# Scores behind the w_in products: one engine order in the last two slots of a period

## The chip, the cores and the metric

The kernel runs on one core of a Trainium2 chip. The core has a matrix engine (TensorE, PE), a vector engine (VectorE, DVE), a scalar engine (ScalarE, ACT), GpSimd (POOL) and SyncE (SP), which issues transfers. Each engine works through its own instructions in the order in which the program gives them, and waits on semaphores where it needs another engine's result. The metric is the time of one execution in microseconds (us); of several executions the median is taken.

## The reference

The input is q, k and v of 8 batches, 8 heads, 576 tokens and 64 dimensions, and the weights w_in (512 x 2048) and w_out (2048 x 512). An approximate attention with 32 landmarks per head is followed by a layer with the activation SiLU:

```python
q_lm = q.reshape(B, H, m, S // m, D).mean(axis=3)      # m = 32 landmarks
k_lm = k.reshape(B, H, m, S // m, D).mean(axis=3)
A, Bm, C = sm(q, k_lm), sm(q_lm, k_lm), sm(q_lm, k)    # softmax of scaled scores
Z = Bm.T / (norm1(Bm) * norminf(Bm) + 1e-06)
for _ in range(6):
    Z = 2 * Z - Z @ Bm @ Z
x = (A @ Z @ C @ v)                                    # heads side by side: 4608 x 512
h = x @ w_in
out = (h / (1 + exp(-h))) @ w_out
```

## The kernel before

The kernel never forms x. For each batch it multiplies the small product Z C v (zwT, 64 x 32 per head) with w_in, which gives a matrix mb of 256 rows and 2048 columns, and then computes h as A times mb. A's softmax needs its scores, which are formed transposed: landmarks against tokens.

The work is cut into eight **periods**, one for each batch b, and each period into sixteen **slots** s. In a slot the kernel forms one sixteenth of h of batch b (`l1_mm`: four matmuls into a tile hps), applies SiLU to it on ScalarE (`l1_act`, line 807, into gT), and runs a few matmuls of the output product (`l2_mm`: ops, 16 matmuls for one block of 128 tokens, then a copy to ost on ScalarE and a transfer). How many ops matmuls a slot gets is written by hand in `CNT` and `REST`. Beside this, a period carries the attention of batch b + 1 (called `a`) through its steps, and prepares batch b + 2 (called `ready`). The schedule is manual: what the program writes first for an engine, that engine does first. The variable d is 2 and 3 in the first two periods and 0 from b = 2 on.

The steps that the change and the prediction touch, for b from 2 to 5:

- Slot 3: a one-word copy on GpSimd (`gate`, line 1139) holds GpSimd until the vector engine has written wsp. After it GpSimd sums landmarks of batch b + 2 (`landmarks_pool`, lines 229 to 237, in slots 4 and 8; the last result is lmn), between them it normalises A (`a_mul`, line 691) and issues the loads of v.
- Slots 7 to 12: four transposes of q and k of batch b + 2 on the vector engine (`transpose_qk`, line 203, into qkT).
- Slots 9 and 14: `a_back` (line 707) transposes the two halves of A of batch b + 1 on the vector engine; the second half is used from slot 8 of the next period.
- Slots 11 and 13: `m_pair` (line 757) forms two of the four column blocks of mb for batch b + 1. Each block is 8 matmuls on 64 x 32 tiles of TensorE. The first block (mp) lies in two banks of PSUM, row half 0 in pool psa and row half 1 in pool psn, and the vector engine casts it (line 773); the second (mpp) lies in a two-bank buffer of pool psh, and ScalarE casts it (line 774).
- Slot 13: `ready = Att(b + 2)` is made, and `lm_t` (line 271) transposes its landmarks lmn into lmc on the vector engine.
- Slot 15: three ops matmuls, then `ready.a_pair` (line 621): 32 score matmuls on 32 x 32 tiles into two psh buffers (sa), two transposes by the vector engine (line 626, into xs) and two reductions for the maxima (line 630, into nm). In slot 0 of the next period GpSimd subtracts them (`a_sub`), and in slot 2 ScalarE takes the exponential.

PSUM is shared out tightly: psh has two buffers of two banks, used in turn by hps, mpp, sa and the scores scp of slot 1; psa and psn have one bank each. psn holds the tile bb of the Newton steps from slot 1 to slot 10 and mp's row half 1 later. A buffer is written again only when its last reader is done.

Of the kernel before, what the change touches and what calls it, by code (L numbers as in the profile page):

```python
# [11 lines left out]
OP = mybir.AluOpType  # L12
AX = mybir.AxisListType
# [30 lines left out]
def kernel(  # L44
# [9 lines left out]
    nc = tc.nc  # L54
    B, H, S, Dh = q.shape
    L = 32
# [187 lines left out]
    class Att:  # L244
# [373 lines left out]
                   .to_broadcast((pr, 8 * n, L)), start=False, stop=True)  # L618


        def a_pair(self):
            self.a_first()
            for i in range(2):
                self.a_scores(i)
            for i in range(2):
                nc.vector.transpose(  # L626
                    out=self.xs[:, i],
                    in_=self.sa[i][:, :, 0:HF].rearrange("p r (t n) -> p r t n", n=L))
            for i in range(2):
                nc.vector.tensor_reduce(out=self.nm[:, i], in_=self.xs[:, i], op=OP.max,  # L630
                                        axis=AX.X, negate=True)
# [122 lines left out]

        def m_pair(self, f):
            self.m_done = f + 2
            if f == 0:
                mb_t[self.b] = attp.tile([128, 2, DFF], BF, tag="mb", name="mb")  # L760
            m = [psa1("mp"), psn1("mp")]
            m2 = ps2("mpp")
            for i in range(2):
                for j in range(4):
                    for r in range(2):
                        p = slice(64 * r, 64 * r + 64)
                        mm((m2[:, r, :] if i else m[r])[32 * j:32 * j + 32, :],
                           self.zwT[p, j, :],
                           w_in_sb[p, j, 512 * (f + i):512 * (f + i) + 512],
                           start=True, stop=True)  # L770
            o = mb_t[self.b][:, :, 512 * f:512 * f + 1024]
            for r in range(2):
                nc.vector.tensor_copy(out=o[:, r, 0:512], in_=m[r])  # L773
            nc.scalar.copy(out=o[:, :, 512:1024], in_=m2)  # L774

# [59 lines left out]
    def l2_add(b, *blocks):  # L837
        for i in blocks:
# [4 lines left out]

    CNT = {0: [0, 0, 0, 0, 4, 4, 2, 4, 4, 4, 2, 2, 2, 2, 1, 1],
           1: [2, 2, 2, 5, 2, 10, 9, 0] + [4] * 8,
           2: [8, 4, 12, 12, 3, 3, 2, 2, 3, 3, 3, 3, 3, 2, 2, 7]}
    REST = [3, 4, 12, 12, 3, 2, 2, 2, 4, 4, 4, 3, 3, 3, 3, 8]


    ORD = (1, 0, 3, 2)  # L850
# [86 lines left out]
    for b in range(B):  # L937
# [4 lines left out]
        a, ready = ready, None  # L942

        d = (2, 3)[b] if b < 2 else 0
        mp = (11, 13) if d == 0 else (14, 15)

        def l1(s):
            h[s] = l1_mm(b, s)
# [4 lines left out]
        for s in range(NDC):  # L953
# [63 lines left out]
            elif s == d + 2 and a.sub:  # L1017
                a.a_start()
                a.c_max(1)
                a.c_exp(0)  # L1020
                a.c_exp(1)
                a.a_exp_all()
                a.b_norm()
                l2_mm(cnt[s])
                table(AF.Silu)
                l1(s)
            elif s == d + 2:
                n = cnt[s]
                a.a_start()
                a.a_scores(0)  # L1030
                a.a_scores(1)
                a.c_max(1)
                a.a_max(0)
                a.a_max(1)
                a.c_exp(0)
                a.c_exp(1)
                a.a_scores(2)
                a.a_max(2)
                for i in range(2):
                    a.a_shift(i)  # L1040
                    a.a_exp(i)
                a.b_norm()
                a.a_shift(2)
                a.a_exp(2)
                table(AF.Silu)
                a0.m_unit(2, nc.vector.tensor_copy, nc.vector.tensor_copy, pair=True)
                a.c_transpose(0)
                a.c_out(0)
                load_v(2)
                a0.a_norm(1)  # L1050
                a0.a_norm(2)
                a.f_mm()
                a.b_scale()
                a.f_out()
                l2_mm(n)
                l1(s)
            elif b == 0:
                l1(s)
                r = s - d
                n = cnt[s]  # L1060
                if r == 3:
                    load_qk(3, (1,))
                    act(s - 1)
                    a0.m_unit(3, nc.scalar.copy, nc.scalar.copy, parts=2,
                              between=lambda: act(s))
                    nc.vector.tensor_tensor(out=parity, in0=mask[:, 0:2, 0],
                                            in1=mask[:, 2:4, 0], op=OP.add)
                elif r == 4:
                    a.ns_mm()
                    a.ns_step()  # L1070
                    act(s)
                    a0.a_transpose(1)
                    a0.a_out(nc.scalar.copy)
                    a.c_transpose(1)
                    a.c_out(1)
                    a.a_norm(0)
                    load_qk(3, (0,))
                elif r == 5:
                    act(s)
                    a.ns_mm()  # L1080
                    a.ns_step()
                    a.w_scale()
                    a.a_norm(1)
                elif r == 6:
                    a.ns_mm()
                    a.ns_step()
                    act(s)
                    l2_mm(2)
                    n -= 2
                    a.ns_mm()  # L1090
                    a.a_norm(2)
                    a.ns_step()
                    load_qk(3, (3,))
                elif r == 7:
                    a.ns_mm()
                    a.ns_step()
                    act(s)
                    l2_mm(2)
                    n -= 2
                    a.w_mm()  # L1100
                    a.w_out()
                    a.ns_mm(last=True)
                    a.x_out()
                    load_qk(3, (2,))
                    landmarks_pool(2, 0)
                elif r == 8:
                    a.z_mm()
                    a.z_out()
                    act(s)
                    l2_mm(n)  # L1110
                    n = 0
                    landmarks_pool(2, 2)
                    a.a_transpose(0)
                    a.a_out(nc.vector.tensor_copy)
                elif r == 10:
                    a.a_transpose(1)
                    a.a_out(nc.vector.tensor_copy)
                    transpose_qk(2, ORD[1])
                elif r > 11:
                    transpose_qk(2, ORD[r - 10])  # L1120
                if s in h:
                    act(s)
                if r in (9, 11):
                    a.m_pair(r - 9)
                if r == 9:
                    transpose_qk(2, ORD[0])
                l2_mm(n)
            elif s == d + 3:
                l1(s)
                act(s - 1)  # L1130
                act(s)
                l2_mm(2)
                a.f_mm()
                a.b_scale()
                a.f_out()
                a.w_scale()


                nc.gpsimd.tensor_copy(out=gate, in_=a.wsp[:, 0, :])  # L1139
                l2_mm(cnt[s] - 2)  # L1140
                a.ns_mm()
            elif s <= d + 8:
                l1(s)
                if s == d + 6:
                    a.w_mm()
                a.ns_step()
                act(s)
                if s == d + 4:
                    a.a_sum(0)
                elif s == d + 5:  # L1150
                    a.a_sum(1)
                elif s == d + 6:
                    a.w_out()
                    a.a_rec(0, 2)
                    a.a_mul(0)
                    a.a_mul(1)
                l2_mm(cnt[s])
                a.ns_mm(last=(s == d + 8))
            elif s == d + 9:
                l1(s)  # L1160
                a.x_out()
                act(s)
                l2_mm(cnt[s])
            elif s == d + 10:
                l1(s)
                a.z_mm()
                a.z_out()
                act(s)
                l2_mm(cnt[s])
            else:  # L1170
                l1(s)
                act(s)
                if nxt and s in mp:
                    a.m_pair(2 * mp.index(s))
                n = cnt[s]
                if s == 15 and ready and ready.early:
                    l2_mm(3)
                    n -= 3
                    ready.a_pair()
                l2_mm(n)  # L1180
            if b == 0:
                if s == 3:
# [1 line left out]
            elif b + 2 < B:  # L1184
# [16 lines left out]
                if s == 15 and b == 1:  # L1201
                    ready = Att(b + 2)
                    ready.lm_t(0, 2)
            back = (9, 14) if d == 0 else (12, 13)
            if nxt and b and s in back:
                a.a_back(back.index(s))
            if (b, s) == (0, 3):
# [34 lines left out]
```

## Time and profile before

| | |
|---|---|
| time, median of 3 executions | 260.57 us |
| lowest and highest | 260.43 and 260.59 us |
| the profiled execution, its own time | 260.7 us |
| its span, first to last instruction | 259.0 us |
| granted clock of TensorE | 1.00 over the whole span |
| mean time of one ops matmul in the records | 373 ns (they overlap; the work's pace is 216 ns) |
| one SiLU of a slot (line 807) | 652 ns |
| one cast of mp on the vector engine (line 773) | 684 ns |
| one cast of mpp on ScalarE (line 774) | 1012 ns |
| one transpose of a score half (line 626) | 762 ns |

The profile is of one execution. Busy time of TensorE counts matmuls that overlap, so it is not a measure of its peak; the pace of a group is read from the starts of its neighbours. In the timeline a line gives the start, the time from the first start to the last end, the engine, the line of the kernel, the tiles (written <- read), the shape, how many instructions are merged, and in brackets the idle time of the engine ahead of it with what ended it. All matmuls are recorded at one helper line, 80, so they are told apart by their tiles. A few per cent of the matmul records can be missing.

### The profile page before, as it was taken

The page shows a single profiled execution, that of the slowest core. Times are in us where ns is not written, and L with a number is a line of the kernel's source. Part 1 is how long each engine was busy: PE and PEld are TensorE (multiplying, and loading weights), DVE is VectorE, ACT ScalarE, POOL GpSimd, SP SyncE. Part 2 cuts the span into 40 slices and gives each one's busy share as a digit, 9 for nine tenths or more (in the row PEclk, how much of TensorE's full clock was granted, in tenths as well). Part 3 has the DMA queues.
Part 4 walks back from the last instruction along what each step waited for, and adds up shares of the span by engine and source line. Part 5 has one row for each costly group of instructions (what it writes and reads, how often), then busy time and mean ns, then how long its engine had stood idle before and what let it go on. Part 6 is the DMA issues. An engine that isn't in the chain of part 4 may idle for free.

```text
span 259.0 us, 6520 instructions
## 1 busy us (share of the span) xinstructions
PE 241.9 (93%) x2676; PEld 137.7 (53%) x2717; DVE 168.3 (65%) x396; ACT 169.9 (66%) x313; POOL 133.2 (51%) x161
## 2 busy tenths in 40 slices
PE   8879878999898999999999999999999999999994
PEld 2646544564554555556655564556545665556553
DVE  5878988769895969777885788776967645000000
ACT  2378964587846786779575957597668858445511
POOL 7707546983799469945993299319923030100000
PEclk9999999999999999999999999999999999999999
DMA  7999999970479982895289518134621500111122
GB/s 221 199 209 208 207 205 211 226 153 10 134 100 235 193 160 52 117 190 142 48 133 192 129 44 132 43 50 94 113 61 44 135 26 25 55 69 41 44 81 82
DMA packets 30062, 31.16 MB, mean 120 GB/s; under 512 B 10960, under 2 KB 21456, under 8 KB 30032
## 3 DMA queue, kind: packets, MB, share of 16 engines
q0 software_dynamic: 14816, 17.76, 42.0%
q1 hardware_dynamic: 15216, 12.98, 17.1%
q8 instruction: 21, 0.34, 0.5%
q14 instruction: 9, 0.07, 0.1%
HBM read 36.70 MB, written 9.44 MB: 178 GB/s over the span
## 4 chain that ended last, share of the span: by engine, by line
PE 77%; DVE 10%; POOL 4%; issue 3%; ACT 3%; DMA 2%; ACTq 0%
PE ops L80 42%; PE hps L80 22%; PE bb L80 3%; PE lmp L80 2%; PE mp L80 2%; PE sa L80 2%; DMA raw<-in_k_dram 2%; DVE cmx L448 2%; PE wp L80 1%; PE scp L80 1%; PE mpp L80 1%; POOL lma L229 1%; DVE nm L609 1%; POOL nat L108 1%; DVE arec L662 1%
## 5 line engine op out<-in xcount | busy, mean ns | idle before, releaser
L80 PE MATMUL ops<-w_out_sb,gT 128*128 128x512 bf16 (+1 forms) x555 | 139.6, 373 | 4.4 <-issue 4.0
L807 ACT ACTIVATE gT<-hps 128x576 bf16<-128x576 f32 (+2 forms) x128 | 82.6, 652 | 56.9 <-PE hps L80 56.1
L80 PE MATMUL hps<-AT,mb 128*128 128x288 bf16 (+2 forms) x512 | 82.8, 286 | 1.2 <-ACT gT L807 0.7
L80 PEld LDWEIGHTS <-gT 128*128 128x128 bf16 x592 | 54.0, 98 | 48.1 <-issue 9.0
L80 PEld LDWEIGHTS <-mb 128*128 128x128 bf16 x512 | 48.4, 97 | 28.1 <-issue 1.9
L203 DVE STREAM_TRANSPOSE qkT<-nat 128x576 f32<-128x576 f32 x32 | 38.8, 1239 | 0.2
L833 ACT COPY ost<-ops 128x512 f32<-128x512 f32 (+1 forms) x37 | 21.1, 570 | 14.3 <-PE ops L80 11.1
L229 POOL TENSOR_TENSOR lma<-nat 128x1152 f32<-128x1152 bf16 x12 | 28.6, 2380 | 0.0
L407 DVE SCALAR_TENSOR_TENSOR fx<-fx,bb 128x320 bf16<-128x320 bf16 (+1 forms) x39 | 17.9, 459 | 11.0 <-PE bb L80 10.9
L773 DVE CAST mb<-mp 128x512 bf16<-128x512 f32 x28 | 18.0, 684 | 7.7 <-PE mp L80 7.7
L635 POOL TENSOR_TENSOR xs<-xs,nm 128x576 f32<-128x576 f32 x12 | 13.6, 1153 | 15.8 <-DVE nm L630 15.8
L165 ACT ACT_TABLE_LOAD x16 | 20.5, 1283 | 1.1 <-PEq L1226 0.8
L80 PE MATMUL bb<-fx 128*128 128x160 bf16 (+2 forms) x132 | 13.5, 212 | 3.6 <-DVE fx L407 1.7
L1139 POOL COPY gate<-wsp 128x2 f32<-128x2 f32 x6 | 1.1, 184 | 30.1 <-DVE wsp L492 30.1
L691 POOL TENSOR_TENSOR an<-ex,arec 128x576 bf16<-128x576 bf16 x12 | 13.6, 1158 | 5.3 <-DVE arec L677 5.3
L80 PEld LDWEIGHTS <-fx 128*128 128x128 bf16 (+1 forms) x132 | 8.4, 94 | 14.1 <-DVE fx L407 5.3
L774 ACT CAST mb<-mpp 128x1024 bf16<-128x1024 f32 x14 | 14.2, 1012 | 0.1
L626 DVE STREAM_TRANSPOSE xs<-sa 128x576 f32<-128x576 f32 x12 | 8.7, 762 | 7.3 <-PE sa L80 7.3
L234 POOL TENSOR_TENSOR lmc<-lmb,lma 128x384 f32<-128x384 f32 x12 | 12.0, 1002 | 0.9
L232 POOL TENSOR_TENSOR lmb<-lma 128x384 f32<-128x384 f32 x12 | 12.0, 998 | 0.9
L448 DVE TENSOR_REDUCE cmx<-scp 128x1 f32<-128x576 f32 x16 | 11.9, 752 | 0.5 <-PE scp L80 0.3
L662 DVE TENSOR_REDUCE arec<-ex 128x18 f32<-128x576 bf16 (+2 forms) x17 | 11.7, 689 | 0.0
(123 smaller groups left out, 261.5 us busy)
## 6 DMA issues: line engine op xcount, KB each, us to landing
out_dram<-ost SPq DMA_DIRECT2D x35, 256.0 KB, 2.0
v<-in_v_dram POOLq DMA_DIRECT2D x8, 576.0 KB, 7.2
nat<-in_k_dram POOLq DMA_DIRECT2D x15, 288.0 KB, 7.1
nat<-in_q_dram POOLq DMA_DIRECT2D x15, 288.0 KB, 8.1
w_in_sb<-in_moe_w_in_dram POOLq DMA_DIRECT2D x4, 512.0 KB, 14.9
w_out_sb<-in_moe_w_out_dram POOLq DMA_DIRECT2D x4, 512.0 KB, 13.9
raw<-in_k_dram SPq DMA_DIRECT2D x1, 576.0 KB, 4.2
raw<-in_q_dram SPq DMA_DIRECT2D x1, 576.0 KB, 5.1
```

The lines of the kernel that those rows point to most:

```text
L80: nc.tensor.matmul(out=o, lhsT=lhsT, rhs=rhs, start=start, stop=stop, skip_group_check=True)
L165: nc.scalar.activation(out=spare[:, 1:2], in_=spare[:, 0:1], func=func)
L203: nc.vector.transpose(out=o.rearrange("p (l t) -> p t l", t=SEG), in_=nat_t[b][:, j, :].bitcast(FP).rearrange("p (t l) -> p t l", l=L))
L229: nc.gpsimd.tensor_tensor(out=a1, in0=nat[:, :, 0:3 * w], in1=nat[:, :, 3 * w:6 * w], op=OP.add)
L407: nc.vector.scalar_tensor_tensor(out=n, in0=self.fx, scalar=2.0, in1=self.p, op0=OP.mult, op1=OP.add if self.tiled else OP.subtract)
L448: nc.vector.tensor_reduce(out=mx, in_=self.s[g][:, :, 0:HF], op=OP.max, axis=AX.XY, negate=True)
L635: nc.gpsimd.tensor_tensor(out=self.xs[:, i], in0=self.xs[:, i], in1=self.nm[:, i].unsqueeze(3).to_broadcast((128, 2, SEG // 2, L)), op=OP.add)
L662: nc.vector.tensor_reduce(out=r, in_=x, op=OP.add, axis=AX.X)
L773: nc.vector.tensor_copy(out=o[:, r, 0:512], in_=m[r])
L774: nc.scalar.copy(out=o[:, :, 512:1024], in_=m2)
L807: nc.scalar.activation(out=gT_t[b][:, 2 * s:2 * s + 2, o + c0:o + c1], in_=h[:, :, 0:c1 - c0], func=AF.Silu)
L833: nc.scalar.copy(out=ost[:, 0:hi - lo], in_=st["ps"][:, 0:hi - lo])
```

## The change

In the periods b = 2 to 5 (batches 4 to 7 are the ones prepared there), the two `m_pair` calls move from slots 11 and 13 to slots 14 and 15. Each takes one half of A's scores with it: behind the 16 matmuls of the pair stand the 16 score matmuls of one half (`a_half`). On the vector engine the cast of mp's row half 0 is followed by the transpose and the reduction of that half (`a_turn`), and only then by the cast of row half 1. In both slots two ops matmuls stand between the slot's hps and the pair. The separate score pair in slot 15 goes. The second `a_back` moves from slot 14 to slot 13. The numbers of ops matmuls in the last two slots become 4 and 5 (b = 2), and 5 and 6 (b = 3, 4, 5 and 7), with the same sum; b = 6 keeps its numbers. In every `m_pair` the cast on ScalarE is now written ahead of those on the vector engine.

```diff
+        def a_half(self, i):
+            if i == 0:
+                self.a_first()
+            self.a_scores(i)
+
+        def a_turn(self, i):
+            nc.vector.transpose(
+                out=self.xs[:, i],
+                in_=self.sa[i][:, :, 0:HF].rearrange("p r (t n) -> p r t n", n=L))
+            nc.vector.tensor_reduce(out=self.nm[:, i], in_=self.xs[:, i], op=OP.max,
+                                    axis=AX.X, negate=True)
...
-        def m_pair(self, f):
+        def m_pair(self, f, other=None):
...
             o = mb_t[self.b][:, :, 512 * f:512 * f + 1024]
+            if other:
+                other.a_half(f // 2)
+            nc.scalar.copy(out=o[:, :, 512:1024], in_=m2)
             for r in range(2):
                 nc.vector.tensor_copy(out=o[:, r, 0:512], in_=m[r])
-            nc.scalar.copy(out=o[:, :, 512:1024], in_=m2)
+                if r == 0 and other:
+                    other.a_turn(f // 2)
...
-           2: [8, 4, 12, 12, 3, 3, 2, 2, 3, 3, 3, 3, 3, 2, 2, 7]}
-    REST = [3, 4, 12, 12, 3, 2, 2, 2, 4, 4, 4, 3, 3, 3, 3, 8]
+           2: [8, 4, 12, 12, 3, 3, 2, 2, 3, 3, 3, 3, 3, 2, 4, 5],
+           6: [3, 4, 12, 12, 3, 2, 2, 2, 4, 4, 4, 3, 3, 3, 3, 8]}
+    REST = [3, 4, 12, 12, 3, 2, 2, 2, 4, 4, 4, 3, 3, 3, 5, 6]
...
-        mp = (11, 13) if d == 0 else (14, 15)
+        both = b > 1 and b + 2 < B
+        mp = (14, 15) if both or d else (11, 13)
...
-                if nxt and s in mp:
+                n = cnt[s]
+                if both and s in mp:
+                    l2_mm(2)
+                    n -= 2
+                    a.m_pair(2 * mp.index(s), ready)
+                elif nxt and s in mp:
                     a.m_pair(2 * mp.index(s))
-                n = cnt[s]
-                if s == 15 and ready and ready.early:
-                    l2_mm(3)
-                    n -= 3
-                    ready.a_pair()
                 l2_mm(n)
...
-            back = (9, 14) if d == 0 else (12, 13)
+            back = (9, 13) if d == 0 else (12, 13)
```

## The prediction

> **What bounds the kernel now.** I read the page's busy shares and its chain first, then the waits of TensorE (PE) in the periods that the change touches (b = 2 to 5, 83 to 194 us), then the timelines of each engine around slots 13 to 15 of b = 3.
>
> ```profile
> PE 241.9 (93%) x2676; PEld 137.7 (53%) x2717; DVE 168.3 (65%) x396; ACT 169.9 (66%) x313; POOL 133.2 (51%) x161
> ...
> PE 77%; DVE 10%; POOL 4%; issue 3%; ACT 3%; DMA 2%; ACTq 0%
> ```
>
> PE is busy almost throughout and carries 77% of the chain. Its waits between 100 and 196 us are one line, and that one is no wait: each such gap follows a packed stretch, and there the weight loads outnumber the matmul records by one, so a record is missing.
>
> ```profile
> PE ops L80 <- issue: 2.2, 14, 0.2
> ```
>
> So here one microsecond of PE time is one microsecond of the kernel, and nothing of it can be hidden. The PE timeline of b = 3, slot 13 to the next period's slot 0:
>
> ```profile
> 132.65 0.65 PE L80 MATMUL hps<-AT,mb 128*128 128x288 bf16 x4
> 133.23 0.41 PE L80 MATMUL mp<-w_in_sb,zwT 64*32 64x512 bf16 x8
> 133.46 0.40 PE L80 MATMUL mpp<-w_in_sb,zwT 64*32 64x512 bf16 x8
> 133.79 0.82 PE L80 MATMUL ops<-w_out_sb,gT 128*128 128x512 bf16 x3
> 134.45 0.65 PE L80 MATMUL hps<-AT,mb 128*128 128x288 bf16 x4
> ...
> 136.07 0.81 PE L80 MATMUL ops<-w_out_sb,gT 128*128 128x512 bf16 x3
> 136.81 0.70 PE L80 MATMUL sa<-qkT,lmc 32*32 32x288 bf16 x32
> 137.67 1.03 PE L80 MATMUL ops<-w_out_sb,gT 128*128 128x512 bf16 x4 [0.16 <-issue]
> 138.53 0.65 PE L80 MATMUL hps<-AT,mb 128*128 128x288 bf16 x4
> ```
>
> An hps group takes (133.79 to 134.45 is three ops at 0.216) 0.49 us of PE time, an ops matmul 0.216. The reader is to see the price of a packed stretch: hps would have ended its turn at 132.65 + 0.49 = 133.14, and ops go on at 133.79, so an m_pair costs **0.65**, of which two groups of 0.226 are work, 0.09 the way in and 0.11 the way out. The score pair: ops' turn ends at 136.07 + 0.65 = 136.72; the four ops recorded from 137.67 are five, so PE was back at 137.67 - 0.22 = 137.45: **0.73**. Half of it, 16 matmuls and the way out, is 0.38.
>
> **The change, part by part.** Everything is counted from t0, the start of slot 14's hps.
>
> *The two m_pairs leave slots 11 and 13*: t0 comes 2 x 0.65 = 1.30 us earlier. Their casts (two on VectorE, DVE, one of 1.01 us on ScalarE, ACT) leave with them; DVE's qkT transpose of slot 12 then runs earlier and is not in the way. What does not move is GpSimd (POOL): from the gate in slot 3 (119.45 in b = 3) it works without a pause to lmn, which ends 133.84; that is 0.61 before t0 today and 0.69 after it then.
>
> *The score pair leaves slot 15*; two joined stretches stand in slots 14 and 15. Unhindered, one is 0.09 in + 0.45 products + x + 0.38 half of the scores, with x the step from 64*32 to 32*32 tiles, which no row of this trace shows. Bounds: 0 (tiled groups among themselves follow at their work's pace) and 0.20 (way in plus way out). I take 0.09, the way in, as the same happens there: the tile shape changes ahead of a packed group. Old: 0.65 + 0.65 + 0.73 = 2.03 per period. New: 2 x (0.92 + x) = 1.84 at x = 0, 2.02 at 0.09. So the gain is 0.19 per period at best and nearly nothing as I take it.
> The Trainium skill, TensorEngine Tiling (Array Packing), Tiling Modes, says that a change of tiling mode, not of the tile alone, drains TensorE. By that rule there are six changes before and six after (in, between, out, twice), and the gain is nothing; by x = 0 it is four periods of 0.19. The rows of the way in and out agree with it; the step between is seen nowhere here.
>
> *The ops counts*: 14 and 15 have 3 + 8 before, 5 + 6 after (b = 2: 2 + 7, 4 + 5); the last period's 3 + 8 become 5 + 6. No matmul is added: nothing. *a_back(1)* goes from slot 14 to 13, in front of the casts on DVE. *ACT's cast* ahead of DVE's in program order: other engine, nothing.
>
> *The order on DVE is the expensive part.* These are DVE's and ACT's rows:
>
> ```profile
> 133.70 1.29 DVE L773 CAST mb<-mp 128x512 bf16<-128x512 f32 x2 [0.48 <-PE mp L80]
> 134.91 0.30 DVE L271 STREAM_TRANSPOSE lmc<-lmn 128x128 f32<-128x128 f32 x1
> 135.14 0.74 DVE L707 STREAM_TRANSPOSE AT<-an 128x576 bf16<-128x576 bf16 x1
> 137.34 1.45 DVE L626 STREAM_TRANSPOSE xs<-sa 128x576 f32<-128x576 f32 x2 [1.46 <-PE sa L80]
> 138.71 1.37 DVE L630 TENSOR_REDUCE nm<-xs 128x18 f32<-128x576 f32 x2
> ```
> ```profile
> 133.34 0.65 ACT L807 ACTIVATE gT<-hps 128x576 bf16<-128x576 f32 x1
> 133.93 1.01 ACT L774 CAST mb<-mpp 128x1024 bf16<-128x1024 f32 x1
> ```
>
> An instruction starts about 0.08 before the one ahead of it ends, or 0.03 after it where it reads its result (bbs at 113.92 behind bmx, which ends at 113.88). New queue of slot 14: cast r0 0.69 - 0.08, transpose 0.76 + 0.03, reduce 0.71 - 0.08, cast r1 0.68: 2.71 from the first cast to the end of the second. mp r1 lies in the one bank of psn, so slot 15's second product waits for that cast; today the two products are two slots apart and nobody waits. When does the first cast start? mp is ready at 0.49 + 2 x 0.216 + 0.09 + 0.48 = 1.49. But lm_t stands ahead of it and waits for lmn:
>
> ```profile
> 106.57 0.45 POOL L237 TENSOR_TENSOR lmn<-lmd,lmc 128x128 bf16<-128x128 f32 x1
> ...
> 133.38 0.46 POOL L237 TENSOR_TENSOR lmn<-lmd,lmc 128x128 bf16<-128x128 f32 x1
> ```
>
> lmn ends, after the new t0, at 1.28, 0.69, 0.67 and 0.66 (b = 2 to 5; 161.63 and 189.43 in the last two). Then 0.03, lm_t 0.23, a_back 0.66: first cast at 2.20, 1.61, 1.59, 1.58. That the wait for lmn can reach PE is to be seen in b = 2's slot 0 (0.03 from lmn to lm_t, 0.06 on to PE):
>
> ```profile
> 82.97 0.31 DVE L271 STREAM_TRANSPOSE lmc<-lmn 128x128 f32<-128x128 f32 x1 [1.08 <-POOL lmn L237]
> 83.34 0.70 PE L80 MATMUL sa<-qkT,lmc 32*32 32x288 bf16 x32 [0.47 <-DVE lmc L271]
> ```
>
> So psn comes free for PE at W = first cast + 2.71 + 0.06: 4.97, 4.38, 4.36, 4.35. Without waits PE would stand there at 0.49 + 0.43 + 0.09 + 0.45 + 0.09 + 0.38 + 0.65 = 2.58 (hps15) and, after 0.49 + 0.43 + 0.09, at 3.59. A second wait lies on that way: both psh buffers are taken by mpp and sa, so hps15 needs ACT's cast of mpp, 1.24 + 0.40 + 0.04 + 1.01 + 0.05 = 2.74. It costs 0.15 and is covered by the longer DVE wait.
>
> From W: products 0.45, x 0.09, scores and way out 0.38, four ops 0.86: next hps at W + 1.79; its buffer needs ACT's second cast, W + 0.23 + 0.40 + 0.04 + 1.01 + 0.05 = W + 1.73, which decides only in b = 2 (three ops: 1.57). Behind that nothing is late: DVE's last cast ends about W + 3.2, its bank is wanted by bb at W + 4.4; nm is ready at W + 2.5, and the exponential that needs it starts 6.05 after slot 0's hps (110.72 to 116.77).
>
> **Sum**, from t0 to the next period's hps: b = 2: 4.97 + 1.73 = 6.70, less 1.30, against 3.67 (107.05 to 110.72): +1.73. b = 3: 6.17 - 1.30 - 4.08 = +0.79; b = 4: +0.76; b = 5: +0.75 (4.09 each). Together +4.03. The profiled execution of 260.7 (span 259.0) would take 264.7; the median of 260.57 becomes **264.6**. Ends: every first cast at 1.49, as if lm_t never waited: +0.65 three times and +1.00, 263.5. x = 0.20 (+0.11 three times) and DVE without its overlap of 0.08 (+0.2 four times): 265.7.
>
> **Rivals.**
> *Gain as it stands* (259.8): no wait reaches PE and x = 0; 4 x 0.19 off. It needs DVE's turn (1.49 + 2.77 = 4.26 at the earliest) to be shorter than PE's way to the second product (3.50 at x = 0); it is 0.76 too long by rows that hardly vary. This is the one on the other side; it decides where the turn is under 2.0 us.
> *The step between tiles eats the gain* (260.5), no wait: x = 0.09. (By the rule of drains in the Trainium skill's TensorEngine Tiling, Tiling Modes, it would be so; no run here shows it.)
> *Only ACT's cast waits* (261.7): psn is free in time, hps15 waits at 2.74 (2.86 in b = 2, where an ost copy stands ahead of the cast): 3 x 0.16 + 0.64 = +1.12.
> *lmn late everywhere*: if POOL is held up as relatively late as in b = 2 in all four, first casts at 2.20: 3 x 1.38 + 1.73, 266.4. POOL's rows are the same in each period, which speaks against it.
>
> **How the numbers follow.** Forecast 0.76, only ACT 0.09, gain 0.06, lmn late 0.05, step between tiles 0.04. The range 261.6 to 265.7 takes in the forecast's ends and the ACT case. A measurement of this kernel can tell about 0.2% (0.5 us) from no change: faster 0.06, same 0.04 (step between tiles), slower 0.90.
>
> **What would show it.** Right: in b = 2 to 5 slot 15's mp group has idle time on PE put down to DVE's cast of mb (line 773 today), about 0.6 us in b = 3 to 5 and 1.1 in b = 2, and t0 comes 1.3 us sooner after its period's first hps. hps15 shows 0.1 to 0.2 behind ACT's cast of mpp; DVE's row reads cast, transpose, reduce, cast without a gap, behind lm_t waiting for lmn. x is the start of sa less that of mpp, less 0.226. Wrong: mp of slot 15 without a wait, a span under 260, or the loss in periods other than these four.

## The result, and the profile after

The changed kernel takes 264.5 us in the median of four executions (264.35 to 265.7), against 260.57 us before: 1.0168 times as long, with a 95% interval of 1.0147 to 1.0188. The profiled execution took 264.53 us, its span is 262.8 us, at a granted clock of 1.00. One execution of all that follow, of the run counts_only, ran at a granted clock of 0.95 and took 266.82 us; it is left out of that run's median.

The page of the changed kernel still shows TensorE at 93% of a longer span, while the chain of what ended last has changed hands:

```profile
PE 243.7 (93%) x2672; PEld 138.0 (53%) x2717; DVE 168.4 (64%) x396; ACT 170.5 (65%) x313; POOL 133.6 (51%) x161
...
PE 43%; POOL 25%; DVE 17%; issue 9%; ACT 3%; DMA 2%; SPq 0%; POOLq 0%; ACTq 0%
```

TensorE's share of the chain was 77%; GpSimd and VectorE now carry 42% of it. In the view of waits (engine and tile, waited for: us in total, times, longest), TensorE from 83 to 200 us had no wait for an engine but the one for lmc; now it has two more (`issue` is a missing record, as before):

```profile
PE mp L80 <- DVE mb L789: 1.5, 4, 0.8
PE ops L80 <- issue: 1.4, 9, 0.2
PE hps L80 <- ACT mb L787: 0.7, 3, 0.2
PE sa L80 <- DVE lmc L271: 0.5, 1, 0.5
```

The 1.5 us of the first line understate it: idle time is counted from the modelled end of the matmul ahead, which reaches past the moment at which the next could have started. The starts in the timeline show the whole of it. TensorE in b = 3, from slot 14 to the next period's slot 0 (hps):

```profile
134.58 0.65 PE L80 MATMUL hps<-AT,mb 128*128 128x288 bf16 x4
135.07 0.59 PE L80 MATMUL ops<-w_out_sb,gT 128*128 128x512 bf16 x2
135.59 0.41 PE L80 MATMUL mp<-w_in_sb,zwT 64*32 64x512 bf16 x8
135.82 0.40 PE L80 MATMUL mpp<-w_in_sb,zwT 64*32 64x512 bf16 x8
136.15 0.45 PE L80 MATMUL sa<-qkT,lmc 32*32 32x288 bf16 x16
136.53 0.60 PE L80 MATMUL ops<-w_out_sb,gT 128*128 128x512 bf16 x2
137.35 0.65 PE L80 MATMUL hps<-AT,mb 128*128 128x288 bf16 x4 [0.22 <-ACT mb L787]
137.84 0.59 PE L80 MATMUL ops<-w_out_sb,gT 128*128 128x512 bf16 x2
138.37 0.39 PE L80 MATMUL mp<-w_in_sb,zwT 64*32 64x512 bf16 x1
138.99 0.41 PE L80 MATMUL mp<-w_in_sb,zwT 64*32 64x512 bf16 x7 [0.24 <-DVE mb L789]
139.01 0.60 PE L80 MATMUL mpp<-w_in_sb,zwT 64*32 64x512 bf16 x8
139.54 0.45 PE L80 MATMUL sa<-qkT,lmc 32*32 32x288 bf16 x16
139.92 1.04 PE L80 MATMUL ops<-w_out_sb,gT 128*128 128x512 bf16 x4
140.80 0.65 PE L80 MATMUL hps<-AT,mb 128*128 128x288 bf16 x4
```

The reader is to see slot 15's mp group torn in two. Its first matmul, into psa, runs at 138.37; the second, into psn, stands until 138.99, 0.62 us. And hps15 comes at 137.35, although its turn was at 136.53 + 3 x 0.216 = 137.18 (three ops matmuls stand there by the program; one record is missing): it waits 0.17 for ScalarE's cast of mpp. VectorE over the same time, with lm_t ahead:

```profile
135.32 0.31 DVE L271 STREAM_TRANSPOSE lmc<-lmn 128x128 f32<-128x128 f32 x1 [2.28 <-POOL lmn L237]
135.55 0.74 DVE L720 STREAM_TRANSPOSE AT<-an 128x576 bf16<-128x576 bf16 x1
136.21 0.65 DVE L789 CAST mb<-mp 128x512 bf16<-128x512 f32 x1
136.79 0.77 DVE L627 STREAM_TRANSPOSE xs<-sa 128x576 f32<-128x576 f32 x1
137.59 0.75 DVE L630 TENSOR_REDUCE nm<-xs 128x18 f32<-128x576 f32 x1
138.26 0.68 DVE L789 CAST mb<-mp 128x512 bf16<-128x512 f32 x1
```

The queue has no gap: lm_t comes when lmn is there, then a_back, cast, transpose, reduction, and the cast that frees psn ends at 138.94, 0.05 before TensorE's second product. In b = 2 the same picture is larger, since lmn comes later there, counted from slot 14's hps at 105.42:

```profile
106.76 0.31 DVE L271 STREAM_TRANSPOSE lmc<-lmn 128x128 f32<-128x128 f32 x1 [2.18 <-POOL lmn L237]
109.22 0.39 PE L80 MATMUL mp<-w_in_sb,zwT 64*32 64x512 bf16 x1
110.43 0.41 PE L80 MATMUL mp<-w_in_sb,zwT 64*32 64x512 bf16 x7 [0.83 <-DVE mb L789]
```

From slot 14's hps to the next period's first hps, less the same stretch before, less what slots 11 to 13 have become shorter by (1.32): 6.76 - 3.67 - 1.32 = 1.77 in b = 2, 6.22 - 4.08 - 1.32 = 0.82 in b = 3, 0.81 in b = 4, 0.78 in b = 5. Together 4.18. The other periods keep their length within 0.02 us, but for the first. The spans differ by 3.8, as this execution reached the first hps of b = 1 at 53.21 us, the one before at 53.53. That is no effect of the change: without it, too, the first period takes 31.3 to 31.8 us, in the profiles of before, before_v12 and before_v0.

### The profile page after: what moved, and what is told of

It reads as the page before. It is cut to its first block, busy times and chain, and to the rows that moved or that the text cites. A ratio compares the mean times of both kernels' runs of the same rounds, so it can differ in the third digit from the quotient of the medians.

```text
span 262.8 us, 6516 instructions
## 1 busy us (share of the span) xinstructions
PE 243.7 (93%) x2672; PEld 138.0 (53%) x2717; DVE 168.4 (64%) x396; ACT 170.5 (65%) x313; POOL 133.6 (51%) x161
## 4 chain that ended last, share of the span: by engine, by line
PE 43%; POOL 25%; DVE 17%; issue 9%; ACT 3%; DMA 2%; SPq 0%; POOLq 0%; ACTq 0%
PE ops L80 23%; PE hps L80 11%; POOL lma L229 8%; POOL lmb L232 3%; POOL lmc L234 3%; POOL an L704 3%; DVE mb L789 2%; DMA raw<-in_q_dram 2%; PE lmp L80 2%; POOL lmd L236 2%; DVE cmx L448 2%; POOL v L114 2%; PE bb L80 1%; DVE nm L630 1%; DVE xs L627 1%
## 5 line engine op out<-in xcount | busy, mean ns | idle before, releaser
L203 DVE STREAM_TRANSPOSE qkT<-nat 128x576 f32<-128x576 f32 x32 | 38.2, 1241 | 0.4 <-POOL nat L154 0.3
L828 POOL COPY gT<-gT 128x1024 bf16<-128x1024 bf16 x4 | 4.2, 1038 | 14.1 <-ACT gT L824 14.1
```

Of the source, the lines that this page charges most:

```text
L203: nc.vector.transpose(out=o.rearrange("p (l t) -> p t l", t=SEG), in_=nat_t[b][:, j, :].bitcast(FP).rearrange("p (t l) -> p t l", l=L))
```

## The experiments

Three theories were set against each other. By the **order theory** TensorE waits for the psn bank, whose cast stands on VectorE behind the transpose and the reduction, which stand behind a_back and the wait for lmn. By the **ACT theory** it is ScalarE's cast of mpp, which holds a psh buffer, that paces the two slots. By the **load theory** VectorE has more work in the two slots than they last, in whatever order. Runs are compared by their ratio to the kernel before on the same chip; the absolute times of the kernel before moved between 260.3 and 260.6.

**casts_first**: both casts ahead of the transpose and the reduction.

```diff
             for r in range(2):
                 nc.vector.tensor_copy(out=o[:, r, 0:512], in_=m[r])
-                if r == 0 and other:
-                    other.a_turn(f // 2)
+            if other:
+                other.a_turn(f // 2)
```

> The changed kernel, with both casts of mp on VectorE ahead of the transpose and the reduction. Order theory (slot 15's products wait for the psn bank because its cast stands behind the turn): the wait of 0.62 us in b = 3 to 5 and 1.22 in b = 2 goes; what stays is hps15 behind ScalarE's cast (0.17 each, 0.26 in b = 2) and in b = 2 the transpose of the score half that mpp's buffer needs (0.2) and the wait for lmc: about 261.8 us. ACT theory (ScalarE's cast of mpp is what paces the two slots): 264 or more, as that cast is where it was. Load theory (VectorE has more work in the two slots than they last, in whatever order): 264.5.

261.53 us, 1.0056 times the kernel before (1.0038 to 1.0074). Two thirds of the loss are gone with one line moved and no work taken away, which neither the ACT theory nor the load theory allows. Slot 15 of b = 3 in this kernel, TensorE:

```profile
136.15 0.65 PE L80 MATMUL hps<-AT,mb 128*128 128x288 bf16 x4
136.63 0.59 PE L80 MATMUL ops<-w_out_sb,gT 128*128 128x512 bf16 x2
137.16 0.41 PE L80 MATMUL mp<-w_in_sb,zwT 64*32 64x512 bf16 x8
137.39 0.40 PE L80 MATMUL mpp<-w_in_sb,zwT 64*32 64x512 bf16 x8
```

The mp group is whole again. What stays is, in b = 3 to 5, the wait of hps15 for ScalarE's cast (0.18 each), and in b = 2 a sum of 0.76: the same wait (0.27), scores behind the late lmn (0.14), mpp behind the transpose of the score half whose buffer it needs (0.20), and the next period's first hps behind ScalarE's second cast (0.17).

**back_14** and **v_later** take away, in two ways, what stands ahead of the first cast.

```diff
-            back = (9, 13) if d == 0 else (12, 13)
+            back = (9, 14) if d == 0 else (12, 13)
```

> The changed kernel with the second a_back in slot 14 again, behind the casts instead of ahead of them. Order theory: the first cast starts with mp's end instead of after a_back, 0.14 us sooner in b = 3 to 5 and 0.66 in b = 2, and the bank comes free so much sooner: 263.4 us. ACT theory: 264.5. Load theory: 264.5, as the transpose is only moved within the two slots.

```diff
-                if s == 7 + d // 2:
+                if s == (7 + d // 2 if d else 9):
                     load_v(b + 2)
```

> The changed kernel with GpSimd's issue of the loads of v (0.85 us on GpSimd) moved from slot 7 to slot 9, behind the last landmark sum, so that lmn ends 0.85 us sooner. Order theory with the wait for lmn ahead of the casts: lm_t and a_back are done before mp is, the first cast starts 0.14 us sooner in b = 3 to 5 and 0.74 in b = 2, and the wait for lmc of 0.14 in b = 2 goes: 263.3 us. ACT theory and load theory: 264.4 to 264.5.

back_14: 263.61 us, ratio 1.0133 (1.0112 to 1.0153). v_later: 263.66 us, 1.0127 (1.0111 to 1.0142). The interval of back_14 overlaps that of the change a little, that of v_later ends just below it, so the periods of the traces are read as well, from first hps to first hps. With the change b = 2 takes 30.93 us and b = 3 to 5 take 28.60 to 28.63. In back_14 it is 30.34 and 28.51, in v_later 30.22 and 28.51: 0.59 and 0.71 less in b = 2, where 0.66 and 0.88 were expected, and 0.09 to 0.12 less in the others, where 0.14 was. VectorE in v_later, in b = 3, now waits for mp, not for lmn:

```profile
134.36 0.74 DVE L720 STREAM_TRANSPOSE AT<-an 128x576 bf16<-128x576 bf16 x1
135.72 0.69 DVE L789 CAST mb<-mp 128x512 bf16<-128x512 f32 x1 [0.63 <-PE mp L80]
```

What stands ahead of the first cast, the wait for lmn with a_back behind it, is thus a part of the loss (about 1 us of 4), the order of the casts the larger one.

**dose_between** and **dose_behind** double the reduction of each half, once between the casts and once behind them.

```diff
         def a_turn(self, i):                      # dose_between
...
+            nc.vector.tensor_reduce(out=self.nm[:, i], in_=self.xs[:, i], op=OP.max,
+                                    axis=AX.X, negate=True)
```

> The changed kernel with each score half's reduction done twice (the second writes the same values), both between the two casts of mp on VectorE. Order theory: the second cast and with it slot 15's products come 0.67 us later in each of the four periods: 4 x 0.67 = 2.7 more than the changed kernel, 267.2 us. Load theory: the same 267.2. ACT theory: 264.5.

```diff
             for r in range(2):                    # dose_behind
...
+            if other:
+                nc.vector.tensor_reduce(out=other.nm[:, f // 2], in_=other.xs[:, f // 2],
+                                        op=OP.max, axis=AX.X, negate=True)
```

> The changed kernel with the same second reduction of each half, but behind the second cast of mp. Order theory: VectorE is done with it about when slot 15's products are, nothing waits: 264.5 to 264.9 us. Load theory: 267.2, as VectorE has the same extra work. ACT theory: 264.5.

dose_between: 267.88 us, ratio 1.0287 (1.0263 to 1.0310); the periods are 0.76 to 0.78 longer than with the change, a little over the 0.67 expected. dose_behind: 264.81 us, 1.0173 (1.0150 to 1.0195), the time of the change. The second product of slot 15 in b = 3, first in dose_between, then in dose_behind:

```profile
138.82 0.39 PE L80 MATMUL mp<-w_in_sb,zwT 64*32 64x512 bf16 x1
140.21 0.41 PE L80 MATMUL mp<-w_in_sb,zwT 64*32 64x512 bf16 x7 [1.00 <-DVE mb L791]
```
```profile
138.51 0.39 PE L80 MATMUL mp<-w_in_sb,zwT 64*32 64x512 bf16 x1
139.13 0.41 PE L80 MATMUL mp<-w_in_sb,zwT 64*32 64x512 bf16 x7 [0.24 <-DVE mb L789]
```

The product stands 1.39 us in the one, and 0.62 in the other, as with the change. The same instruction costs three quarters of a microsecond per period ahead of the cast and nothing behind it. That is the load theory's end: VectorE had room for it.

**counts_only**: the kernel before with the new numbers of ops matmuls and a_back in slot 13, products and scores where they were (the diff is that of CNT, REST and back alone).

> The kernel before with only the new numbers of ops matmuls in slots 14 and 15 and the second a_back in slot 13; products and scores stay where they were. Order theory, ACT theory and load theory: no difference, 260.5 to 260.7 us. If the numbers or a_back's place carry a part of the loss: 261 or more.

261.18 us, ratio 1.0038 (1.0025 to 1.0052): all theories missed. With the score pair still in slot 15, three ops matmuls instead of five stand behind it (two instead of four in b = 2), and the next hps, which needs the psh buffer of the first half, meets VectorE's transpose. The counts-only kernel at the end of b = 2, TensorE and VectorE:

```profile
109.28 0.70 PE L80 MATMUL sa<-qkT,lmc 32*32 32x288 bf16 x32
109.91 0.61 PE L80 MATMUL ops<-w_out_sb,gT 128*128 128x512 bf16 x2
110.63 0.65 PE L80 MATMUL hps<-AT,mb 128*128 128x288 bf16 x4
...
107.60 0.73 DVE L707 STREAM_TRANSPOSE AT<-an 128x576 bf16<-128x576 bf16 x1
109.80 1.45 DVE L626 STREAM_TRANSPOSE xs<-sa 128x576 f32<-128x576 f32 x2 [1.46 <-PE sa L80]
```

Two ops end their turn at 109.91 + 0.43 = 110.34, hps comes at 110.63, 0.28 later; 0.07 in b = 3 to 5. The moved a_back (line 707) has no part in it: it ends 0.95 us ahead of the scores. Another 0.10 is lost in slot 4 of b = 3 to 6, where hps waits for ScalarE, whose exponentials, and the SiLU behind them, ran 0.10 later in the period. That begins on VectorE: bbs, an instruction of 0.17 us in most periods, takes 0.43 to 0.44 there and ends 0.02 to 0.03 behind GpSimd's subtraction of the maxima, which ran beside it. The counts therefore belong to the move of the scores: in the changed kernel, where half of the scores have gone to slot 14, slots 0 to 10 have their old length (18.99 us in b = 4 and 5).

**scores_first**: the joined stretch the other way round, scores ahead of products; VectorE: transpose, cast, cast, reduction; the loads of v in slot 9.

```diff
+            if other:
+                other.a_half(f // 2)
             m = [psa1("mp"), psn1("mp")]
...
-            if other:
-                other.a_half(f // 2)
             nc.scalar.copy(out=o[:, :, 512:1024], in_=m2)
+            if other:
+                other.a_shift_t(f // 2)      # the transpose of a_turn
             for r in range(2):
                 nc.vector.tensor_copy(out=o[:, r, 0:512], in_=m[r])
-                if r == 0 and other:
-                    other.a_turn(f // 2)
+            if other:
+                other.a_low(f // 2)          # the reduction of a_turn
```

> The changed kernel with the two parts of each joined stretch exchanged (scores, then products), VectorE's order transpose, cast, cast, reduction, and the loads of v issued in slot 9. Then hps15 needs the transpose's buffer and not ScalarE's cast, and psn's cast ends 0.5 us before slot 15's products want the bank. Order theory: no wait is left and the step between the tile shapes (0.10, read from the changed kernel's starts) eats what the dropped way in and out saves: 260.5 us, no gain over the kernel before. If the step cost nothing in this direction: 259.8. Load theory: 264 or more.

260.48 us, ratio 0.9995 (0.9983 to 1.0006): the waits in slots 14 and 15 are gone, and the kernel is where it was before the change (its periods b = 3 to 5 take 27.83 us, before 27.81). On TensorE every start in the two slots of b = 3 follows from the work ahead of it; slot 14:

```profile
133.99 0.45 PE L80 MATMUL sa<-qkT,lmc 32*32 32x288 bf16 x16
134.37 0.41 PE L80 MATMUL mp<-w_in_sb,zwT 64*32 64x512 bf16 x8
134.59 0.40 PE L80 MATMUL mpp<-w_in_sb,zwT 64*32 64x512 bf16 x8
134.93 0.82 PE L80 MATMUL ops<-w_out_sb,gT 128*128 128x512 bf16 x3
```

From sa to mp 0.38 us pass. The 16 score matmuls are 0.26 of it: from sa to the ops behind it are 0.64 us in counts_only, where sa has 32 matmuls, and 0.38 in the changed kernel, where it has 16. So the step costs 0.12 in this direction, as much as the way out of the scores (0.38 - 0.26) and a little more than the 0.10 from products to scores. That the stretches touch is worth nothing in sum, with all else out of the way.

**scores_apart**: the same with two ops matmuls between scores and products (an `l2_mm(2)` behind `a_half`, two fewer behind the stretch).

> The kernel scores_first with two ops matmuls, taken from those behind the stretch, between scores and products, so that the two no longer touch. Each of the eight stretches then pays a way out and a way in (0.20) in place of the step between tile shapes. With a step of 0.10: 8 x 0.10 = 0.8 us over scores_first. With a free step: 1.6 over. With a step of 0.20 (a full way out and in): the same time as scores_first.

261.37 us, ratio 1.0047 (1.0028 to 1.0066). In the traces the periods of b = 3 to 5 are 28.04 us against 27.83, 0.21 for two stretches, as a step of 0.10 has it; b = 2 is 0.41 longer, 0.18 of it because slot 15's scores wait there for ScalarE's cast. So touching does save one way in and out, less one step, and the change needed that saving just to pay for having split the score pair in two.

**first_v12** and **before_v12** came from a wait that both kernels share: 0.47 us in slot 0 of b = 2, scores behind lmc behind lmn. In b = 1 the loads of v were issued later, on top of scores_first and of the kernel before.

```diff
-                if s == 7 + d // 2:
+                if s == (12 if d else 7):     # first_v12: (12 if d else 9)
                     load_v(b + 2)
```

> The kernel scores_first, and in period b = 1 the loads of v issued by GpSimd in slot 12, behind its last landmark sum, in place of slot 8. In scores_first one wait of PE for a result of GpSimd is left, 0.46 us in slot 0 of b = 2 (scores behind lmc, behind lmn); lmn should end 0.82 us sooner and that wait go. If GpSimd's row is what holds lmn there: 260.0 us, 0.46 under scores_first and under the kernel before. If lmn is held by something else (its loads, say), or the wait is made up for elsewhere: 260.5.

> The kernel before with only that move of the loads of v in b = 1. If GpSimd's row holds lmn there: the wait of 0.47 us in slot 0 of b = 2 goes, 260.1 us, the same gain as in first_v12, since the order in the later periods has no part in it. If not: 260.5.

263.31 us, 1.0107 (1.0080 to 1.0134), and 263.06 us, 1.0089 (1.0055 to 1.0124): slower, against the expectation. The wait did go (slot 0 of b = 2 is 0.55 shorter in before_v12), but a new and longer one came in slot 6 of b = 2; in the profiled executions the whole period is 1.6 and 1.5 us longer. before_v12, TensorE:

```profile
97.85 0.36 PE L80 MATMUL wp<-v,eCT 96*32 96x64 bf16 x24 [1.60 <-DMA eCT<-eC]
98.44 0.36 PE L80 MATMUL wp<-v,eCT 96*32 96x64 bf16 x24 [0.23 <-DMA eCT<-eC]
```

The transposing transfers of eCT, issued at 88.6 and 90.0 us, landed after 8.4 to 9.2 us; in the kernel before it was 4.1 to 4.8. The loads of v now left GpSimd together with the four loads of q and k (82 to 85 us) and were still under way.

**first_v0** and **before_v0**: the same loads in slot 0 of b = 1, where GpSimd waits for the maxima anyway.

```diff
-                if s == 7 + d // 2:
+                if s == (0 if d else 7):      # first_v0: (0 if d else 9)
                     load_v(b + 2)
```

> The kernel scores_first, and in period b = 1 the loads of v issued in slot 0, where GpSimd otherwise waits for the vector engine, in place of slot 8. lmn of slot 15 again ends 0.82 us sooner, and the loads run while the transfer queues are nearly idle (58 to 65 us) and not beside the transposing transfers of b = 2, which in the move to slot 12 landed after 8.4 to 9.2 us in place of 4.1 to 4.8 and held PE for 1.8 us. If that collision was what the move to slot 12 cost: 260.0 us, 0.46 under scores_first. If moving the loads of v at all is what costs: 261 or more.

> The kernel before with only that move of the loads of v in b = 1 to slot 0. If the collision was the cost of slot 12: 260.1 us, 0.47 under the kernel before. If not: 261 or more.

first_v0: 259.73 us, 0.9962 (0.9947 to 0.9977). before_v0: 259.99 us, 0.9975 (0.9959 to 0.9991). The transfers of eCT land in 3.0 to 3.7 us in before_v0, and the view of waits lists none of TensorE between 80 and 196 us. Both are faster than the kernel before and than the change; between the two the intervals overlap, and the traces give their later periods 27.83 and 27.81 us, so the order of scores and products has no part in the gain.

## Why the prediction was right

- **The wait that sets the time.** Slot 15's second product was forecast at W = 4.97, 4.38, 4.36 and 4.35 us after slot 14's hps. In b = 2 it is 110.43 - 105.42 = 5.01, in b = 3 138.99 - 134.58 = 4.41. casts_first and the pair of doses show that it is the order of VectorE's queue, and not its load, that puts it there.
- **The wait ahead of it.** First cast forecast at 2.20 in b = 2 and 1.61 in b = 3, measured 2.23 and 1.63. back_14 and v_later take it away in two ways and come out within 0.1 us of each other.
- **The step between tile shapes** was taken at 0.09; sa starts 0.33 after mpp, of which 0.226 are mpp's work: 0.10. The Trainium skill's rule that a change of tiling mode drains the array (TensorEngine Tiling (Array Packing), Tiling Modes) had this side of it: three steps per stretch, six per period before and after. The runs agree in both directions, 0.10 and 0.12 (scores_first), and scores_first shows the sum: no gain. That an array drains there is the skill's account; the runs show the price alone.
- **The terms of the sum.** +1.73, 0.79, 0.76, 0.75 were forecast; +1.77, 0.82, 0.81, 0.78 measured. The small excess in each is in W, which came 0.03 to 0.07 later than worked out; from W to the next hps it is 0.01 to 0.02 more, and slots 11 to 13 became 0.02 shorter than the 1.30 forecast. That the time came within 0.1 us of the forecast 264.6 is partly luck: the terms were 0.15 too small in sum, and the profiled execution reached b = 1 0.3 us sooner than the one before.
- **ScalarE's cast** was held to cost 0.15 and to be covered. It does hold hps15 back by 0.17, and casts_first shows what it is worth once uncovered: of the 1.30 us by which the four periods stay longer there, the waits for this cast are 0.98.
- **"The ops counts: nothing"** holds inside the change only. Alone they cost 0.4% (counts_only): in the kernel before the ops behind the score pair were the cover for VectorE's transpose, and the prediction did not name that cover. It cost the forecast nothing, as the change takes the pair away with it.

## What to carry to other kernels

Before a producer is moved up to its successor, ask for each buffer it fills who empties it, and what stands ahead of that reader in its own queue; a reader that is off the chain can set the pace once two fillings come closer together than one turn of its queue, here 2.8 us. When work is interleaved on the reader's engine, put first what frees the scarcest bank. And price a joined stretch by its steps: here a step from one tile shape to another cost 0.10 to 0.12 us, as much as a way out (0.11 to 0.12) and no less than a way in (0.09), so that joining what had been one piece elsewhere saved nothing.

## What the runs showed of the hardware that was not expected

The transposing transfers of eCT, issued by SyncE, landed only after the loads that GpSimd had issued before them, although they are on another queue (q1, the loads on q0). In three kernels the last of the four loads of q and k that stand ahead of them lands at 93.15 us (before), 97.12 (before_v12) and 90.93 (before_v0), and the first transfer of eCT, issued between 88.2 and 89.2 us in each, at 94.04, 97.81 and 91.84: 0.7 to 0.9 us behind it every time. In before_v12 not one packet of q1 started between the issue at 88.6 us and 92.5, while those of q0 kept the 16 transfer engines busy; from then on both queues moved. Whether the transposing transfers wait for their turn or only for free engines, no run separates. So 0.6 MB of loads, issued 10 us later (82.0 in place of 72.1 us), moved a result that they have nothing to do with, and held TensorE for 1.8 us in slot 6.
